# Attention backward on one core: dQ one group later, and other places for the turns of dQ, dK and dV

## The chip, the core and the metric

The kernel runs on one core of one Trainium2 chip, as one launch. The metric is the device time of that launch in microseconds. The core has five engines that run in parallel, each from its own queue of instructions: PE (TensorE, matrix multiplications), ACT (ScalarE, exponentials and copies), DVE (VectorE, elementwise work), POOL (GpSimd) and SP (SyncE, here a queue that issues DMAs). PE writes to PSUM, which the engines read from there; everything else that is computed on lies in SBUF. [...]

## The reference

The reference runs a transformer block with adaptive layer norm forward (S = 2048 tokens, D = 512, H = 32 heads of 16, an MLP with F = 1792) and returns its output and the gradients of nine inputs. What matters here is the gradient of the attention:

```python
scores = jnp.einsum('bhqd,bhkd->bhqk', q, k) * scale
p = _softmax(scores, axis=-1)
o = jnp.einsum('bhqk,bhkd->bhqd', p, v)
...
_out, _vjp = jax.vjp(_f, A_x, A_wqkv, ...)
_grads = _vjp(grad_out)
```

For each head, with P the softmax and dO the gradient of o, the backward pass needs dV = P^T dO, dP = dO V^T, dS = P * (dP - rowsum), dQ = scale * dS K and dK = scale * dS^T Q. The row sums enter through extra columns of dO and V, and the reciprocals of the softmax's sums are folded into dO, so that the kernel uses exp(scores) in place of P.

## The kernel before

The kernel has a forward part, a backward loop over the attention (`attn_bwd`, from about 1166 us to 2390 us of the profiled span) and a last part with the weights' gradients and the gradient of the input. The order in which PE and SP get their instructions is the program's own order, written out by hand; in the backward loop the same holds for POOL.

**Loops.** The backward loop runs over 16 pairs of heads: `g` from 0 to 7 (four heads each) and `jp` 0 or 1. Within a pair, `c` runs over four chunks of 512 keys, `ib0` over four blocks of four query tiles, and `i` over the four tiles of 128 queries in a block. One (`c`, `ib0`) is called a group here, and `m` (0 to 15) is its number within the pair; there are 256 groups in all. One (group, `i`) is a unit.

**A unit.** PE computes the scores of both heads (L1586, into a `st` tile of PSUM, three of them), ACT takes the exponential (L1589, into `pu`, six of them). One unit later, PE computes dP (L1511, into `dp`, three PSUM tiles) and DVE multiplies it by `pu` (L1515) into `ds`, of which there are three, each for one group. In groups with an odd `m` (`off`), one of the eight products is done otherwise: ACT copies dP to SBUF (L1523) and POOL multiplies (L1524). Units then wait in the list `pend`, and some units later `kv` adds their parts of dK and dV on PE into the single PSUM tile `acckv` (L1455). At the end of each chunk `c` ACT evicts `acckv` to `kvT` (L1458).

**dQ.** dQ needs dS transposed. When the last unit of a group is in `ds`, SP issues a DMA that transposes the group into a `dsT` buffer (L1532); in groups with an even `m`, four of its 32 blocks are transposed by PE at `i == 2` of the group itself and copied over by ACT instead (`turn_ds`, L1545 and L1546). There are four `dsT` buffers. The group's eight dQ steps (a step is four matmuls of `dq`, L1478, into the PSUM tile `accq`) go into the list `pendq`, which is served at `i == 0` and `i == 2` of each group:

```python
elif i % 2 == 0 and len(pendq) > 4 * G:
    for _ in range(8 if len(pendq) > 6 * G else 4):
        dq(pendq.pop(0))
```

With G = 4, a group's steps join the list at `i == 0` of the next group, and are worked off at `i == 0` and `i == 2` of the third group after it. After a pair's last step DVE evicts `accq` to `dqT` (L1483); the next pair's first dQ step writes the same PSUM tile.

**Turns.** At the end of a pair dK and dV lie in `kvT`, and dQ in `dqT`, with the head's elements along the partitions. A turn transposes them on PE and copies them to their places on ACT: for dK and dV two turns, each of eight transposes (L1468) and two copies (L1472); for dQ one turn of four transposes (L1491) and one copy (L1492). Turns wait in the list `turnq`; at `i == 3` of any group one of them is taken, if there is one. So a pair's turns are done in the first groups of the next pair.

**Loads.** POOL's queue brings the heads' next K, Q, V and dO in pieces (L1575), about one in each group, after a small copy (`tick`, L1574) that waits for the latest `ds`. In the last two pairs the pieces are weights and the normed input for the part after the loop.

Of the kernel before, what the change touches and what calls it, by code (L numbers as in the profile page):

```python
# [105 lines left out]
class K:  # L106
# [1322 lines left out]
    def attn_bwd(self):  # L1429
# [8 lines left out]
        S, D, H, NQ, ST, SC = self.S, self.D, self.H, self.NQ, self.ST, self.SC  # L1438
        G = 4
# [7 lines left out]
        pend, pendq, turnq = [], [], []  # L1447
# [12 lines left out]
        def turn(g, jp, kvT, s0):  # L1460

            if kvT is None:
                return turn_q(g, jp)
            h0 = 4 * g + 2 * jp
            n = ST // 2
            tp = stp.tile([P, n, P], BF16, name="st")
            for st in range(n):
                nc.tensor.transpose(tp[:, st, :], kvT[:, (s0 + st) * P:(s0 + st + 1) * P], self.ident[:])  # L1468
            v = tp[:].rearrange("p s (t a e) -> p t s a e", t=2, a=2)
            for t, dst in enumerate((self.dk_t, self.dv_t)):  # L1470
                d = dst[:, s0:s0 + n, h0 * DH:(h0 + 2) * DH].rearrange("p s (a d) -> p s a d", a=2)
                nc.scalar.copy(d, v[:, t, :, :, 0:DH])  # L1472

        def dq(u):
            (T, g, jp, c, ib0, a, sub, dsT) = u
            col = 32 * (2 * jp + a) - DH * a
            for i in range(G):
                nc.tensor.matmul(accq[32 * i:32 * i + 32, ib0 // G, :], lhsT=T["K"][:, 4 * c + sub, col:col + 32],  # L1478
                                 rhs=dsT[:, (i * 2 + a) * 4 + sub, :],
                                 start=(c == 0 and ib0 == 0 and a == 0 and sub == 0), stop=False,  # L1480
                                 skip_group_check=True)
            if (c, ib0, a, sub) == (SC - 1, ST - G, 1, 3):
                nc.vector.tensor_scalar(self.dqT[:], accq[:].rearrange("p b q -> p (b q)"), self.scale, None, ALU.mult)  # L1483
                turnq.append((g, jp, None, 0))
# [9 lines left out]
        def kv_two(n=2):  # L1494
            for _ in range(n):
                u = pend.pop(0)
                kv(u)
                (T, g, jp, c, ib, kvT, pu, ds) = u
                if ib < ST - 1:
                    continue  # L1500
                if c % 2 and (g, jp) == (NQ - 1, 1):
                    turnq.append((g, jp, kvT, 4 * (c - 1)))
                elif c == SC - 1:
                    turnq.extend((g, jp, kvT, s0) for s0 in (0, ST // 2))

        def dP(u, a):

            (T, g, jp, c, ib, kvT, pu, dsg, i, grp) = u
            rd = slice(64 - 64 * jp, 128 - 64 * jp)
            dp = dpp.tile([P, 512], F32, name="dp")  # L1510
            nc.tensor.matmul(dp[:], lhsT=T["dOT"][rd, ib * P:(ib + 1) * P],  # L1511
                             rhs=masked["VT"][a][rd, 512 * c:512 * (c + 1)], start=True, stop=True)
            if a == 1 and i == 1 and off(c, ib):
                return dp
            nc.vector.tensor_tensor(dsg[:, i, a], dp[:], pu[:, a, :], ALU.mult)  # L1515

        def off(c, ib):
            return (c * SC + ib // G) % 2 == 1

        def dP_pool(u, dp):  # L1520
            (T, g, jp, c, ib, kvT, pu, dsg, i, grp) = u
            f = (self.junk6, self.csq)[(c * SC + ib // G) // 2 % 2]
            nc.scalar.copy(f[:], dp[:])  # L1523
            nc.gpsimd.tensor_tensor(dsg[:, i, 1], f[:], pu[:, 1, :], ALU.mult)  # L1524

        def dS(u):

            (T, g, jp, c, ib, kvT, pu, dsg, i, grp) = u
            pend.append((T, g, jp, c, ib, kvT, pu, dsg[:, i]))
            if i == G - 1:  # L1530
                dsT, n = grp
                nc.sync.dma_start_transpose(dsT[:, n:, :], dsg[:].rearrange("p i a k -> p (i a k)")[:, n * P:])  # L1532
                for a in range(2):
                    for sub in range(4):
                        pendq.append((T, g, jp, c, ib - G + 1, a, sub, dsT))

        def turn_ds(dsg, grp, skip):

            dsT = dtp.tile([P, 8 * G, P], BF16, name="dsT")
            grp.extend((dsT, 0 if skip else 4))  # L1540
            if skip:
                return
            tp = stp.tile([P, 4, P], BF16, name="st")
            for b in range(4):
                nc.tensor.transpose(tp[:, b, :], dsg[:, 0, 0, b * P:(b + 1) * P], self.ident[:])  # L1545
            nc.scalar.copy(dsT[:, 0:4, :], tp[:])  # L1546
# [4 lines left out]
        for g in range(NQ):  # L1551
            for jp in range(2):
                if jp == 0:
                    if g + 1 < NQ:
                        Tn, later = self.load_group(g + 1)
                    else:
                        Tn, later = None, self.wq_pieces(1) + self.load_wmt()
                    cut = len(later) // 2 if Tn else len(later)
                    pieces = self.pair_pieces(g, 1) + later[:cut]
                    later = later[cut:]  # L1560
                elif g + 1 < NQ:
                    pieces = self.pair_pieces(g + 1, 0) + later
                else:
                    pieces = [(self.xhat1_6[:, st, :], self.xhat1_d.rearrange("(st p) d -> p st d", p=P)[:, st, :])
                              for st in range(ST)]
                kvT = kvp.tile([P, S], BF16, name="kvT")
                total = len(pieces)
                for c in range(SC):
                    c0 = 512 * c
                    for ib0 in range(0, ST, G):  # L1570
                        m = c * (ST // G) + ib0 // G
                        while pieces and (total - len(pieces)) * SC * ST <= m * G * total:
                            if last:
                                nc.gpsimd.tensor_copy(tick[:], last[7][0:1, 0, 0, 0:1])  # L1574
                            nc.gpsimd.dma_start(*pieces.pop(0))  # L1575
                        dsg, grp = self.dsp.tile([P, G, 2, 512], BF16, name="ds"), []
                        for i in range(G):
                            ib = ib0 + i
                            q = slice(ib * P, (ib + 1) * P)
                            if turnq and i == 3:  # L1580
                                turn(*turnq.pop(0))
                            pu = self.pup.tile([P, 2, 512], BF16, name="pu")
                            for a in range(2):
                                stt = stp.tile([P, 512], F32, name="st")
                                rs = slice(64 * jp, 64 * jp + 64)
                                nc.tensor.matmul(stt[:], lhsT=T["QT"][rs, q], rhs=masked["KT"][a][rs, c0:c0 + 512],  # L1586
                                                 start=True, stop=True)
                                held = dP(last, a) if last else None
                                nc.scalar.activation(pu[:, a, :], stt[:], ACT.Exp, scale=self.scale)  # L1589
                                if held is not None:  # L1590
                                    dP_pool(last, held)
                                if a == 0 and i % 2 == 1 and off(c, ib) and len(pend) >= 4:
                                    kv_two(1)
                            if last:
                                dS(last)
                            last = (T, g, jp, c, ib, kvT, pu, dsg, i, grp)
                            if i % 2 == 1 and len(pend) >= 4:
                                kv_two(1 if off(c, ib) else 2)
                            elif i % 2 == 0 and len(pendq) > 4 * G:
                                for _ in range(8 if len(pendq) > 6 * G else 4):  # L1600
                                    dq(pendq.pop(0))
                            if i == 2:
                                turn_ds(dsg, grp, off(c, ib))
            T = Tn
# [341 lines left out]
```

## Time and profile before

| | |
|---|---|
| runs of the kernel before | 2515.72 us median of 3 (2510.71 to 2517.65) |
| the profiled execution's own time | 2515.11 us |
| its span in the trace | 2513.3 us, 76903 instructions |
| granted TensorE clock | 0.998 of full speed |
| PE, ACT, DVE, POOL busy | 97%, 91%, 68%, 28% of the span |
| the backward loop | 1166 to 2390 us, about 76.5 us a pair |

Busy shares are of the whole span, and are no measure of one stage: DVE is at 68% overall, and at 9 tenths or more in every slice of the backward loop. A row of the groups of instructions gives the line, the engine, what is written from what, the count, the busy time and the mean duration, and then the idle time of the engine just before such instructions, with the instruction whose end released it. Durations of instructions in a row on ACT and DVE overlap, so that the distance from start to start is shorter than the duration. A wait row gives the waiting engine and line, what it waited for, the sum, the number of waits and the longest. A DMA's row on SP shows how long its issue took there; the time to landing is shown separately.

### The profile page before, as it was taken

How to read it: one execution, taken by the hardware profiler on the slowest of the kernel's cores; microseconds unless marked ns; L12 is line 12 of the kernel's file. 1: busy time of each engine (PE TensorE's matmuls, PEld its weight loads, DVE VectorE, ACT ScalarE, POOL GpSimd, SP SyncE). 2: the span in 40 equal slices, each digit the busy share in tenths (PEclk: the TensorE clock that was granted, in tenths of full speed). 3: DMA queues.
4: the chain of work that ended last, by engine and by line, in shares of the span. 5: the costliest groups of instructions: out<-in, count | busy, mean ns of one | idle time of the engine just before them, and what ended most of it. 6: DMA issues, size and time to landing. Idle time of an engine off the chain costs nothing.

```text
span 2513.3 us, 76903 instructions
## 1 busy us (share of the span) xinstructions
PE 2437.6 (97%) x30791; PEld 1133.6 (45%) x30791; DVE 1708.5 (68%) x3519; ACT 2297.0 (91%) x3773; POOL 715.9 (28%) x1289
## 2 busy tenths in 40 slices
PE   8999999999999999999999999999999999999998
PEld 4555555555555554673333333333333333333343
DVE  6222323422332333677999999999999999999957
ACT  7999999999999997535999999999999999999935
POOL 2344531321131022255222222222222222222223
PEclk9999999999999999999999999999999999999999
DMA  4589661441343044699999999999999999999997
GB/s 166 135 180 206 173 117 67 112 100 45 102 118 75 24 134 134 133 203 210 233 225 218 219 228 221 228 227 219 221 221 226 227 224 219 227 224 231 237 191 205
DMA packets 1260558, 446.30 MB, mean 178 GB/s; under 512 B 1204052, under 2 KB 1228246, under 8 KB 1260198
## 3 DMA queue, kind: packets, MB, share of 16 engines
q1 hardware_dynamic: 1219654, 336.29, 71.5%
q0 software_dynamic: 38464, 104.04, 13.7%
q8 instruction: 241, 3.95, 0.6%
q10 hardware_dynamic: 2080, 1.05, 0.1%
q14 instruction: 119, 0.97, 0.1%
HBM read 75.83 MB, written 64.49 MB: 56 GB/s over the span
## 4 chain that ended last, share of the span: by engine, by line
PE 55%; ACT 24%; DMA 12%; issue 4%; DVE 3%; POOL 0%; SPq 0%; DVEq 0%; ACTq 0%; POOLq 0%
ACT pu L391 19%; PE st L1586 15%; DMA dsT<-ds 10%; PE st L388 8%; PE acckv L1455 7%; PE accq L1478 5%; ACT pu L1589 4%; PE accbank L322 3%; DVE ds L1515 2%; PE dps L1050 2%; PE pps L1237 2%; PE dp L1511 1%; PE st L1545 1%; PE dps L995 1%; PE pps L631 1%
## 5 line engine op out<-in xcount | busy, mean ns | idle before, releaser
L1515 DVE TENSOR_TENSOR ds<-dp,pu 128x512 bf16<-128x512 f32 x1920 | 1180.5, 684 | 33.2 <-PE dp L1511 26.4
L1589 ACT ACTIVATE pu<-st 128x512 bf16<-128x512 f32 x2048 | 1075.3, 657 | 34.6 <-PE st L1586 21.3
L391 ACT ACTIVATE pu<-st 128x1024 bf16<-128x1024 f32 x992 | 912.1, 1077 | 2.9 <-PE st L388 2.7
L388 PE MATMUL st<-QTm,KTq 128*128 128x512 bf16 x1984 | 587.7, 377 | 19.5 <-ACT pu L391 6.0
L322 PEld LDWEIGHTS <-pu 128*128 128x128 bf16 x8192 | 347.5, 96 | 235.7 <-issue 2.5
L1511 PE MATMUL dp<-kvm,q 64*128 64x512 bf16 x1024 | 363.5, 384 | 1.3 <-DVE g2w L1056 0.7
L1511 PE MATMUL dp<-kvm,dOTg 64*128 64x512 bf16 x1024 | 362.2, 384 | 0.0
L322 PE MATMUL accbank<-Vaug,pu 128*128 128x17 bf16 x8192 | 357.7, 171 | 1.2 <-ACT Vaug L522 0.9
L1586 PE MATMUL st<-kvm,q 64*128 64x512 bf16 x1024 | 349.9, 381 | 4.7 <-ACT pu L1589 0.2
L1586 PE MATMUL st<-kvm,QTg 64*128 64x512 bf16 x1024 | 349.4, 381 | 4.0
L388 PEld LDWEIGHTS <-KTq 128*128 128x128 bf16 x1984 | 188.1, 96 | 176.1 <-issue 124.4
L1524 POOL TENSOR_TENSOR ds<-junk,pu 128x512 bf16<-128x512 f32 x64 | 73.9, 1154 | 370.3 <-ACT junk L1523 284.1
L1455 PE MATMUL acckv<-ds,Qg 128*16 128x512 bf16 x1024 | 176.2, 382 | 0.0
L1455 PE MATMUL acckv<-pu,dOg 128*16 128x512 bf16 x1024 | 175.9, 382 | 0.0
L1455 PE MATMUL acckv<-pu,q 128*16 128x512 bf16 x1024 | 175.8, 382 | 0.0
L1455 PE MATMUL acckv<-ds,q 128*16 128x512 bf16 x1024 | 175.8, 382 | 0.0
L1524 POOL TENSOR_TENSOR ds<-csq,pu 128x512 bf16<-128x512 f32 x64 | 73.8, 1153 | 354.5 <-ACT csq L1523 354.5
L302 POOL DMA_DIRECT2D QTm<-QTq_d x124 | 63.3, 512 | 340.8 <-PE st L388 320.0
L1586 PEld LDWEIGHTS <-q 64*128 64x128 bf16 x1024 | 66.9, 93 | 141.0 <-issue 108.8
L1586 PEld LDWEIGHTS <-QTg 64*128 64x128 bf16 x1024 | 66.6, 93 | 141.0 <-issue 108.0
L329 DVE RECIPROCAL rl<-accbank 128x4 f32<-128x4 f32 x128 | 23.0, 179 | 157.4 <-PE accbank L322 157.2
L1478 PE MATMUL accq<-dsT,Kg 128*32 128x128 bf16 x4096 | 105.5, 221 | 10.5 <-DMA dsT<-ds 10.2
(387 smaller groups left out, 3168.2 us busy)
## 6 DMA issues: line engine op xcount, KB each, us to landing
KTq<-KTq_d POOLq DMA_DIRECT2D x24, 512.0 KB, 3.7
duT_d<-auT POOLq DMA_DIRECT2D x3, 1792.0 KB, 7.7
aT_d<-rT POOLq DMA_DIRECT2D x3, 1792.0 KB, 11.1
KTq_d<-KTq SPq DMA_DIRECT2D x32, 128.0 KB, 2.2
QTq_d<-ev_fm SPq DMA_DIRECT2D x32, 128.0 KB, 4.3
ktm_d<-ev_tm POOLq DMA_DIRECT2D x32, 128.0 KB, 2.6
VTq_d<-vT POOLq DMA_DIRECT2D x4, 1024.0 KB, 6.3
dsT<-ds SPq DMA_TRANSPOSE x256, 6.9
```

Source lines behind the costliest of these rows:

```text
L302: nc.gpsimd.dma_start(QTm[j][32 * j:32 * j + 32, :], self.QTq_d[g, 32 * j:32 * j + 32, 512 * qc:512 * (qc + 1)])
L322: nc.tensor.matmul(acc[:, a, sub, :], lhsT=pu[:, a, sub * P:(sub + 1) * P], rhs=Vaug[:, kb, h, :], start=(kb == 0 and a == 0 and sub == 0) ...
L388: nc.tensor.matmul(stt[:, a, :], lhsT=KT[:, kb * P:(kb + 1) * P], rhs=QTm[2 * jp + a][:], start=True, stop=True)
L391: nc.scalar.activation(pu[:], stt[:], ACT.Exp, scale=self.scale)
L1050: nc.tensor.matmul(pt[:], lhsT=a[st], rhs=g_tm[:, st, :], start=(st == 0), stop=(st == ST - 1))
L1455: nc.tensor.matmul(acckv[r:r + DH, :], lhsT=T[n][:, ib, col:col + DH], rhs=src[:, a, :], start=(ib == 0), stop=(ib == ST - 1))
L1478: nc.tensor.matmul(accq[32 * i:32 * i + 32, ib0 // G, :], lhsT=T["K"][:, 4 * c + sub, col:col + 32], rhs=dsT[:, (i * 2 + a) * 4 + sub, :], ...
L1511: nc.tensor.matmul(dp[:], lhsT=T["dOT"][rd, ib * P:(ib + 1) * P], rhs=masked["VT"][a][rd, 512 * c:512 * (c + 1)], start=True, stop=True)
L1515: nc.vector.tensor_tensor(dsg[:, i, a], dp[:], pu[:, a, :], ALU.mult)
L1524: nc.gpsimd.tensor_tensor(dsg[:, i, 1], f[:], pu[:, 1, :], ALU.mult)
L1586: nc.tensor.matmul(stt[:], lhsT=T["QT"][rs, q], rhs=masked["KT"][a][rs, c0:c0 + 512], start=True, stop=True)
L1589: nc.scalar.activation(pu[:, a, :], stt[:], ACT.Exp, scale=self.scale)
```

## The change

A variable `lag` takes the place of the constant 4 in the rule for `pendq`: it is 6 in all pairs but the last, where it stays 4. With 6, a group's dQ steps are worked off in the fourth group after it instead of the third. The number of `dsT` buffers stays four. In the last pair, the first two groups have steps of eight in place of four until the list is down to its old length.

A turn is taken only from a certain group of the pair on: one of dK and dV from `m` = 2, one of dQ from `m` = 7. Before, the dK and dV turns came at `m` = 1 and 2 (the last `kv` of a pair is done at `i == 3` of the next pair's group 0), and the dQ turn at `m` = 3; now they come at 2, 3 and 7. Since dQ itself ends a group later, the eviction of `accq` moves from `m` = 2 to `m` = 3.

```diff
                 kvT = kvp.tile([P, S], BF16, name="kvT")
+                lag = 4 if (g, jp) == (NQ - 1, 1) else 6
                 total = len(pieces)
...
-                            if turnq and i == 3:
+                            if turnq and i == 3 and m >= (7 if turnq[0][2] is None else 2):
                                 turn(*turnq.pop(0))
...
                             if i % 2 == 1 and len(pend) >= 4:
                                 kv_two(1 if off(c, ib) else 2)
-                            elif i % 2 == 0 and len(pendq) > 4 * G:
-                                for _ in range(8 if len(pendq) > 6 * G else 4):
+                            elif i % 2 == 0 and len(pendq) > lag * G:
+                                for _ in range(8 if len(pendq) > (lag + 2) * G else 4):
                                     dq(pendq.pop(0))
```

## The prediction

> **What bounds the kernel now.** I read the page's busy shares first (PE 97%, ACT 91%, DVE 68%), then its slices: from slice 18 on PE, DVE and ACT all show 9, so the backward loop, about 1166 to 2390 us, is the stretch to look at. Within it a table of windows gives, of 1220 us, PE 1195, ACT 1205 and DVE 1186 busy. Then the groups of instructions:
>
> ```profile
> L1515 DVE TENSOR_TENSOR ds<-dp,pu 128x512 bf16<-128x512 f32 x1920 | 1180.5, 684 | 33.2 <-PE dp L1511 26.4
> L1589 ACT ACTIVATE pu<-st 128x512 bf16<-128x512 f32 x2048 | 1075.3, 657 | 34.6 <-PE st L1586 21.3
> ...
> L1478 PE MATMUL accq<-dsT,Kg 128*32 128x128 bf16 x4096 | 105.5, 221 | 10.5 <-DMA dsT<-ds 10.2
> ```
>
> Columns: busy us and mean ns | idle before, with its releaser. DVE and ACT each have one large group and almost no idle time; the reader should notice that what idles them comes from PE, and that PE itself is idle for a DMA at L1478. The waits of PE, ACT and DVE inside the loop (us, times, longest):
>
> ```profile
> PE accq L1478 <- DMA dsT<-ds: 15.1, 29, 1.3
> ...
> ACT pu L1589 <- PE dp L1511: 8.1, 15, 1.2
> ...
> DVE ds L1515 <- PE dp L1511: 26.3, 56, 1.2
> ```
>
> dQ waiting for its transposed dS is PE's only wait with a named cause. By windows it is 9.9 us up to 2231, 2.7 in the pair from 2231 to 2309 (pair 15) and 2.5 in the last pair. The tile view of dsT:
>
> ```profile
> L1532 SPq DMA_TRANSPOSE dsT<-ds x256: 3433/4162/6181, 1173.0 to 2389.8; - x128
> ...
> DMA to landing us min/median/max: 5.3/6.9/9.7
> ```
>
> From starts in the trace: the first dQ matmul of a group comes 8.1 us (median) after the issue of its transpose. A landing of up to 9.7 us misses that: this is the 1.3 us of lateness.
>
> Next the turns, in ACT's timeline of one pair (start, length, what). L1546 and L1523 are the one copy that each group makes at i = 2, so from one to the next is one group:
>
> ```profile
> 1626.19 0.59 ACT L1546 COPY dsT<-st 128x512 bf16<-128x512 bf16 x1
> ...
> 1631.06 0.70 ACT L1523 COPY junk<-dp 128x512 f32<-128x512 f32 x1
> 1631.53 0.51 ACT L1472 COPY dk_t<-st 128x256 bf16<-128x256 bf16 x1
> ...
> 1636.11 0.62 ACT L1546 COPY dsT<-st 128x512 bf16<-128x512 bf16 x1
> 1636.58 0.43 ACT L1472 COPY dk_t<-st 128x256 bf16<-128x256 bf16 x1
> ...
> 1641.29 0.59 ACT L1523 COPY csq<-dp 128x512 f32<-128x512 f32 x1
> 1641.75 0.62 ACT L1492 COPY dq_t<-st 128x512 bf16<-128x512 bf16 x1
> ...
> 1646.58 0.59 ACT L1546 COPY dsT<-st 128x512 bf16<-128x512 bf16 x1
> ```
>
> and DVE at the same place:
>
> ```profile
> 1631.74 4.97 DVE L1515 TENSOR_TENSOR ds<-dp,pu 128x512 bf16<-128x512 f32 x8 [0.58 <-PE dp L1511]
> 1636.63 0.68 DVE L1483 TENSOR_SCALAR dqT<-accq 128x512 bf16<-128x512 f32 x1
> 1637.23 4.27 DVE L1515 TENSOR_TENSOR ds<-dp,pu 128x512 bf16<-128x512 f32 x7
> 1641.85 2.58 DVE L1515 TENSOR_TENSOR ds<-dp,pu 128x512 bf16<-128x512 f32 x4 [0.36 <-PE dp L1511]
> ```
>
> So today the turns fall in groups 1 and 2 (dK, dV) and 3 (dQ). The three intervals are 5.05, 5.18 and 5.29 us; the same places later in the pair take 4.49, 4.62 and 4.67 (copies at 1651.45, 1655.94, 1660.56, 1665.23). The turns cost 0.56, 0.56 and 0.43 (0.62 less a DMA wait of 0.19), 1.55 us a pair; ACT's share by start-to-start distances is 0.53, 0.53 and 0.48. In group 1 DVE idles 0.58 for the turn. In group 2 it does not, because the eviction of accq (L1483, +0.60 from its start to the next) stands in the same place.
>
> Even groups give DVE 8 multiplications, odd ones 7 (the eighth goes to POOL). At 0.598 us from start to start that is 4.78 and 4.19; ACT has 8 x 0.478 + 0.466 = 4.29 in either. DVE binds even groups, ACT odd ones.
>
> **What the Trainium skill says.** "Perfetto Trace Analysis", Identifying the Most-Contended Engine: matmul busy share is no measure, for Scalar and Vector occupancy is; hence I use ACT and DVE, and the trace bears it out, since PE's 97% still leaves its stalls to reach both. Same page, Optimizing Scalar/DVE Operations: an instruction's profiled time overlaps the next one's by its write acknowledgement; here 684 ns against a distance of 598 (L1515), 657 against 478 at the tightest (L1589), so I count distances. Same page, Summary of the profiler window: of a hardware-queue DMA the window leaves out the data movement; here 4.16 us on SP against 6.9 to landing. "DMA: Bandwidth & Descriptors", Issuing engines are not separate DMA queues: loads from another queue interleave on the same 16 engines. The trace agrees: the last two pairs, with the largest loads, have 5.2 us of waits in 154, against 9.9 in the 1065 before.
>
> **The change part by part.** Nothing is added or removed on any engine. The built instruction order has SP and POOL unchanged, dQ one group later on PE, the turns' copies moved on ACT, the eviction L1483 moved on DVE.
>
> *dQ one group later.* The deadline of a landing goes from 8.1 to 8.1 + 4.6 = 12.7 us; the longest recorded is 9.7. So PE's wait ends in all pairs but the last, where the lag is 4 as today: 15.1 - 2.5 = 12.6 us. How much reaches the end: the 256 groups took 14 us more in sum than if each had taken the median of its place in the pair; 14/15.1 = 0.93, so 11.7. What is late next: the ds ring of three. DVE's first write into a reused ds buffer also waits for that transpose, and comes 1.0 us after dQ did, at 9.1 us. Two of 64 recorded landings are above 9.1, and with the longest wait at 1.3 little is left: I give back 0.9 (none to 3). **-10.8.** The dsT ring: the buffer is freed by dQ at i = 2 and taken by L1546 at the same i = 2; the copy follows transposes that stand behind that dQ on PE, so ACT's exponentials behind it wait for nothing new. POOL's loads of K come in the second pair of a group from its group 4 on, the last dQ of the old K ends in group 3 of the first: no wait. Both at nothing.
>
> *Catching up in the last pair.* Groups 0 and 1 hold 4 more dq steps each, 16 matmuls that take 0.34 us from start to next start. The first pair has one group less of them, where PE is not the limit. Between 0 and 0.7; **+0.3.**
>
> *Turns and eviction.* Group 1 loses its turn: -0.56. The dK/dV turn in group 2 now stands alone, in a DVE-bound group where ACT has 4.62 - 4.29 = 0.33 to spare: between 0.2 and 0.53, I take 0.25. In group 3 the second turn stands beside the eviction, as group 2 has it today: 0.56 (0.15 if the eviction fills DVE's idle time in an odd group and the turn ACT's spare time). The dQ turn in group 7 is as in group 3 now: 0.43 (0.1 to 0.48). New sum 0.25 + 0.52 + 0.43 = 1.2, taking 0.52 for group 3 as the odd group is lighter for DVE; gain 0.35 a pair (0 to 1.1). There are 15 pairs with turns; the last keeps its eviction in group 2, so 14.5: **-5.1** (+1 to -13).
>
> Sum -15.6. Against the profiled execution's own 2515.1 (span 2513.3 and 1.8 around it) that gives 2499.5; the median of the runs is 0.6 higher, so 2500.
>
> **Rivals.** *The turns gain nothing*: each costs its ACT time wherever it stands. For: they cost 0.56 and 0.43 now, near their full 0.53 and 0.48, even where ACT had slack. Against: those places had no DVE backlog. 2515.7 - 10.5 = 2505.
>
> *The wait moves to the ds ring, or the transposes are short of rate and not of time*, so a later deadline only lets them fall further behind. For: DMA slices at 9 throughout. Against: SP itself waits for DVE before 219 of the 256 transposes, which a queue with a backlog would not. Turns and catch-up alone: 2515.7 - 4.8 = 2511.
>
> *Slower*: the eviction in front of the next pair's dQ, now between groups 3 and 4. Today L1483 ends 0.95 us before that dQ starts. With both a turn and the seven multiplications ahead, it decides once DVE falls a further 0.95 us behind PE; then PE waits up to the eviction's 0.68 in each of 15 pairs, and the turn in group 2, with no cover, idles DVE 0.58: 1.26 x 15 = 19, less 10.8: 2524. Against it: the odd group is the one where DVE has most room.
>
> *The change does not do what it says* is excluded by the instruction order.
>
> **Numbers.** Both parts as summed 0.64; turns at nothing 0.20; ds ring or rate 0.12; slower 0.04. A measurement of this kernel tells about 0.3%, 7.5 us, from no change: faster means below 2508.2. That takes 0.62 + 0.19 + 0.03 = 0.84; within 0.3% 0.12; slower 0.04. Range: from DMA at 12.6 and turns at 12 (2491) to the ds-ring case (2510).
>
> **What would show it.** Right: PE's wait at L1478 falls to about 2.5 us, nearly all after 2300; DVE's idle time falls with it; intervals of groups 1, 2, 3 and 7 near 4.5, 4.9, 5.2 and 5.1. Wrong: a wait of DVE at L1515 for a dsT landing (ds ring); a wait of PE at L1478 on L1483 (slower rival); intervals of 2, 3 and 7 longer by the full 0.5 each.

## The result, and the profile after

The changed kernel takes 2526.19 us (median of 18 runs, 2515.53 to 2543.11) against 2516.44 for the kernel before (18 runs, 2510.71 to 2527.45): a ratio of 1.004, 95% interval 1.0023 to 1.0057. It is some 10 us slower, where 16 less were forecast, and its runs scatter more. Its profiled execution took 2524.76 us, with a span of 2522.6.

The two large groups on the page of the changed kernel (busy us, mean ns | idle before, releaser):

```profile
L1515 DVE TENSOR_TENSOR ds<-dp,pu 128x512 bf16<-128x512 f32 x1920 | 1181.2, 682 | 42.3 <-DMA dsT<-ds 16.5
L1590 ACT ACTIVATE pu<-st 128x512 bf16<-128x512 f32 x2048 | 1072.6, 661 | 28.2 <-PE st L1587 22.1
```

The work is what it was. What is new is DVE's releaser: it was PE's dP and is now the landing of a transpose. The waits in the changed kernel's loop up to 2385 us, of PE, then DVE, then ACT (us, times, longest):

```profile
PE dp L1511 <- DVE ds L1515: 14.3, 25, 1.6
...
DVE ds L1515 <- DMA dsT<-ds: 16.5, 24, 2.0
DVE ds L1515 <- PE dp L1511: 12.4, 45, 0.6
...
DVE ds L1515 <- PE acckv L1455: 3.2, 6, 0.6
DVE ds L1515 <- PE st L1587: 2.8, 3, 1.2
...
ACT dsT L1546 <- PE st L1545: 14.1, 22, 2.2
```

PE's wait at L1478, 15.1 us before, is gone from this list. In its place DVE waits 16.5 us for the same transposes, where it wants to write into a ds buffer that one of them still reads. PE then waits for DVE, and ACT waits for PE: L1546, the copy that each even group makes at `i == 2`, needs PE's transposes of the group's first ds slice, which is the very slice that DVE could not write. ACT's only row in the kernel before was 8.1 us; now L1546 alone has 14.1.

The 16.5 us are not all of it. By the trace DVE waits at the first write into a group's ds buffer in nine more places, 5.9 us in sum, which the view puts down to PE (all six at `acckv`, two of the three at L1587) or, once, to ACT. Where the landing of the transpose concerned is recorded, in one of the nine, DVE starts 0.12 us after it, just as it does in the seven recorded waits that the view puts down to the DMA. Taken as landings too, these make 22.4 us in 33 waits.

One such place, in the timeline of DVE and then of ACT:

```profile
2033.90 2.58 DVE L1515 TENSOR_TENSOR ds<-dp,pu 128x512 bf16<-128x512 f32 x4
2038.16 3.68 DVE L1515 TENSOR_TENSOR ds<-dp,pu 128x512 bf16<-128x512 f32 x6 [1.69 <-DMA dsT<-ds]
```

```profile
2034.01 4.28 ACT L1590 ACTIVATE pu<-st 128x512 bf16<-128x512 f32 x8
2039.98 0.58 ACT L1546 COPY dsT<-st 128x512 bf16<-128x512 bf16 x1 [1.70 <-PE st L1545]
2040.47 1.09 ACT L1590 ACTIVATE pu<-st 128x512 bf16<-128x512 f32 x2
```

DVE idles 1.69 us for a landing and ACT 1.70 us behind it: here the wait passes through whole. The exponentials that stand behind L1546 in ACT's program start only after it, at 2040.47. The tile view of dsT in the changed kernel (issue on SP in ns, min/median/max; then landing):

```profile
L1532 SPq DMA_TRANSPOSE dsT<-ds x256: 3482/4368/6627, 1175.7 to 2403.3; - x128
...
DMA to landing us min/median/max: 5.4/7.6/10.2
```

The median issue went from 4162 to 4368 ns and the median landing from 6.9 to 7.6 us. From the trace: the mean issue is 4.26 us before and 4.53 now, and of the 256 transposes 57 before and 154 now were issued over 0.15 us after their last product on DVE was ready, because SP was still at the one before. So the transposes are not only waited for elsewhere: they come later. By the trace the loop, from the first to the last exponential, is 1221.9 us before and 1232.6 now.

The delay of the issue is what the ds ring has no room for. Counted from the issue, two of the 64 recorded landings are above 9.1 us, the same number as before. Counted from the end of the group's last product on DVE, which an issue in time follows by 0.06 us, 15 of the 64 are above 9.15 us, against 3 before. Of the 33 transposes that DVE waited for, 30 were issued late, and the mean delay of all 33 is 1.2 us.

### The profile page after: what moved, and what is told of

Its sections match the earlier page's. It is cut to its first block, busy times and chain, and to the rows that moved or that the text cites. A ratio compares the mean times of both kernels' runs of the same rounds, so it can differ in the third digit from the quotient of the medians.

```text
span 2522.6 us, 76901 instructions
## 1 busy us (share of the span) xinstructions
PE 2449.2 (97%) x30791; PEld 1130.8 (45%) x30791; DVE 1710.2 (68%) x3519; ACT 2298.4 (91%) x3773; POOL 714.0 (28%) x1289
## 4 chain that ended last, share of the span: by engine, by line
PE 54%; ACT 24%; DMA 13%; issue 4%; DVE 3%; POOL 1%; SPq 0%; DVEq 0%; ACTq 0%; POOLq 0%
ACT pu L391 18%; PE st L1587 15%; DMA dsT<-ds 11%; PE st L388 8%; PE acckv L1455 7%; ACT pu L1590 4%; PE accq L1478 4%; PE accbank L322 3%; PE dps L1050 2%; PE dp L1511 2%; PE pps L1237 2%; DVE ds L1515 1%; PE st L1545 1%; PE dp L1640 1%; PE pps L631 1%
## 5 line engine op out<-in xcount | busy, mean ns | idle before, releaser
L1515 DVE TENSOR_TENSOR ds<-dp,pu 128x512 bf16<-128x512 f32 x1920 | 1181.2, 682 | 42.3 <-DMA dsT<-ds 16.5
L1587 PE MATMUL st<-kvm,q 64*128 64x512 bf16 x1024 | 349.7, 381 | 4.6 <-ACT pu L1590 0.2
L1587 PE MATMUL st<-kvm,QTg 64*128 64x512 bf16 x1024 | 350.2, 383 | 3.9
L1587 PEld LDWEIGHTS <-QTg 64*128 64x128 bf16 x1024 | 66.7, 94 | 142.0 <-issue 108.8
L1587 PEld LDWEIGHTS <-q 64*128 64x128 bf16 x1024 | 66.9, 93 | 141.3 <-issue 109.2
L1511 PEld LDWEIGHTS <-q 64*128 64x128 bf16 x1024 | 89.7, 93 | 53.0 <-issue 46.1
```

## The experiments

Each ratio is to the kernel before, run on the same chip in between, with its 95% interval. "Loop" is the stretch from the first to the last exponential in the profiled execution.

### The two parts alone

dQ one group later, with the old rule for turns:

```diff
-if turnq and i == 3 and m >= (7 if turnq[0][2] is None else 2):
+if turnq and i == 3:
```

> dQ one group later, turns where they were (groups 1, 2, 3). Theory R (the transposes are short of rate; the later dQ takes away the wait of PE that kept them apart, they queue up on SP, and the wait comes back on DVE at the ring of three ds buffers): as slow as the changed kernel, 2520 to 2530 us against 2516, with over 10 us of DVE waiting at L1515 for dsT, and a mean issue of a transpose on SP above 4.4 us (4.26 before, 4.53 in the changed kernel). Theory T (the new places of the turns cost the time): faster than before, about 2505, since the waits at L1478 are gone and the turns are the old ones.

Measured: 2527.09 us, ratio 1.0039 (1.0026 to 1.0053). And the new turns with dQ in the third group:

```diff
-lag = 4 if (g, jp) == (NQ - 1, 1) else 6
+lag = 4
```

> Turns in groups 2, 3 and 7, dQ in the third group after its own as before. Theory R: no change, 2516 within 4 us; PE waits about 15 us at L1478 for dsT, DVE does not wait for it, the mean issue on SP stays near 4.26 us. Theory T: slower, 2522 to 2530 us.

Measured: 2517.67 us, ratio 1.000 (0.9988 to 1.0013), with PE's wait for dsT at 11.8 us, none of DVE, and a mean issue of 4.26 us. With dQ where it was, no cost or gain of the new places of the turns is seen within that interval; the time of the first run is as theory R had it.

Its mechanism is not. Without the new places of the turns DVE waits only 2.2 us for dsT, or 4.6 with the four waits at a first write that the view puts down to PE, where theory R had over 10; the mean issue is 4.36 us. PE's waits in the loop of the kernel with the later dQ alone show another cause, and DVE's row for dsT follows them:

```profile
PE st L1491 <- DVE dqT L1483: 15.2, 14, 1.1
PE dp L1511 <- DVE ds L1515: 3.4, 8, 0.8
...
DVE ds L1515 <- DMA dsT<-ds: 2.2, 5, 0.7
```

With dQ a group later, `accq` is evicted in group 3, and its turn follows at `i == 3` of that same group: PE stands before L1491 until DVE gets to L1483, 1.1 us in each of 14 pairs. (Group 3 takes 5.86 us from copy to copy in the median, 4.87 before.) Before, the dQ turn was third in the queue of turns and came a group later. So the rule `m >= 7` belongs to the later dQ: it takes this wait away. The 0.99 us by which group 3 is longer makes about 14 us in 14 pairs. Different causes stood behind the two equal times, and the totals alone would have hidden that.

### A fourth ds buffer

If the ring of three ds buffers is what is short, a fourth should free the loop. It takes 8 KB per partition, which are not free; they were first won by loading WmT after the loop. The control is the kernel before with that load moved, without the last two lines below.

```diff
...
-later = None, self.wq_pieces(1) + self.load_wmt()
+later = None, self.wq_pieces(1)
...
 wk = self.wkp = self.open_pool("p6w", bufs=1, side="right")
+for piece in self.load_wmt():
+    nc.gpsimd.dma_start(*piece)
...
-self.dsp = self.open_pool("p5ds", bufs=3)
+self.dsp = self.open_pool("p5ds", bufs=4)
```

> Control for the next run: the kernel before, but WmT (1.5 MB in 8 pieces) is loaded after the loop instead of in pair 15, into a pool of the last part, which leaves 12 KB per partition free in the loop. Every theory: waits at L1478 in pair 15 fall from 2.7 us towards 1, the last part may lose up to 5 us; 2511 to 2521.

> The changed kernel with WmT loaded after the loop, and four ds buffers instead of three. Theory N (the ring of three ds buffers alone is what is short; the transposes are late now and then but have rate enough): both deadlines are now above 12 us, no wait for dsT in the loop, 2500 to 2505. Theory R: transposes stay queued on SP with a mean issue of 4.5 us or more, DVE or PE still waits for dsT over 8 us in all, and the time is not below 2512.

Measured: the control 2524.1 us, ratio 1.0021 (1.0011 to 1.0032), worse than expected; the changed kernel with four buffers 2515.89, ratio 0.9993 (0.998 to 1.0006). The totals mix two things. The loop of the latter is 1206.3 us, 15.6 less than before, and PE's waits in it are nearly nothing; DVE has none for dsT:

```profile
PE accq L1478 <- DMA dsT<-ds: 1.6, 2, 1.4
PE dp L1511 <- DVE ds L1515: 0.7, 3, 0.3
```

But the part after the loop grew from 125.0 us to 132.9 in the control and 138.9 here, where the late load stands beside other transfers; in the twelve traces with WmT loaded in the loop it takes 120.0 to 128.9 us. So the forecast gain of the loop is there once ds has four buffers, and is given back by WmT. Of theory R one half stays true here: the mean issue is 4.44 us and 170 transposes were issued late. They queue, but with both deadlines above 12 us (dQ 12.0 and the ds ring 13.4 us after the issue, in the median) it no longer matters.

### The same fourth buffer without moving WmT

WmT's tile is empty until pair 15, so up to there every fourth group can use a view of it as its ds buffer. The first call of `load_wmt` makes the tile alone; its pieces are issued in pair 15 as before.

```diff
...
+self.load_wmt()
+ds4 = self.WmT[:].rearrange("p a b c -> p (a b c)")[:, 0:G * 1024].rearrange("p (i a k) -> p i a k", i=G, a=2)
...
-dsg, grp = self.dsp.tile([P, G, 2, 512], BF16, name="ds"), []
+fourth = m % 4 == 3 and g < NQ - 1
+dsg, grp = ds4 if fourth else self.dsp.tile([P, G, 2, 512], BF16, name="ds"), []
```

> The changed kernel with a fourth ds buffer that costs no memory: up to group 7's pairs every fourth group uses a view of WmT's tile, which is loaded in pair 15 as before. Theory N (what holds the changed kernel back is the ring of three ds buffers: the transposes are later than before, but have rate enough): no wait for dsT up to 2230 us, the loop at about 1208 us as with four buffers and WmT loaded late (1206), and the last part as before: 2500 to 2505 us against 2517, at least 18 below the changed kernel. Theory D (the late load of WmT had relieved the loop, not the buffer): 2515 to 2525, with waits of DVE for dsT as in the changed kernel.

> The same fourth ds buffer in the kernel before, dQ in the third group. Theory N: no change, 2517 within 4 us, since dQ's deadline of 8.1 us is met or missed before that of the ds ring (9.1); PE's wait at L1478 stays at 10 to 16 us. If a longer ds ring helps by itself (theory B), PE's wait falls below 8 us and the time below 2510.

Measured: 2532.4 us, ratio 1.0064 (1.004 to 1.0088), in the changed kernel, and 2551.89, ratio 1.0137 (1.0114 to 1.0159), in the kernel before. Neither theory had that. The tile view of dsT in the former, out of the pool's buffers and out of the view:

```profile
L1535 SPq DMA_TRANSPOSE dsT<-ds x200: 3471/4440/6384, 1174.9 to 2409.7; - x100
...
L1535 SPq DMA_TRANSPOSE dsT<-WmT x56: 4882/5432/7137, 1188.9 to 2252.9; - x56
```

The shortest issue out of the view took 4882 ns. Groups with m = 1, 5, 9, 13 move as many blocks and took 4.90 us on average, those of the view 5.39. The built program has the three ds buffers at multiples of 512 bytes, and the view at 188384, which is 32 bytes short of one. The next two runs move its start by 16 elements, in the line that makes `ds4`:

```diff
-[:, 0:G * 1024]
+[:, 16:16 + G * 1024]
```

> As ring4, but the view begins 32 bytes further on, so that it starts at a multiple of 512 bytes like the three ds buffers (in ring4 it did not, and a transpose out of it took 5.2 to 5.5 us on SP against 4.2 to 5.0). Theory N with alignment: the extra length of those transposes goes, no wait for dsT before 2230 us but in the first pair, loop about 1208 us, total 2500 to 2505. Theory A (alignment does not matter, the place in SBUF does, or the fourth buffer itself): 2525 to 2535 as ring4.

> The aligned fourth ds buffer with dQ in the third group and the old turns. Theory N: 2517 within 4 us with PE's wait at L1478 between 10 and 16 us, since dQ's deadline comes before that of the ds ring. Theory B (a longer ring helps by itself): below 2508.

Measured: 2511.02 us, ratio 0.9965 (0.9952 to 0.9978), with the later dQ; 2522.18, ratio 1.0015 (1.0004 to 1.0025), with dQ in the third group. The view's transposes in the former:

```profile
L1535 SPq DMA_TRANSPOSE dsT<-WmT x56: 4084/4990/6566, 1188.2 to 2230.1; - x56
```

The view's transposes are now like the others: up to pair 14 they take 5.00 us on average, and those of m = 1, 5, 9, 13 take 5.05. With dQ in the third group, where fewer stand queued, the view's mean went from 5.19 to 4.38 us, and that of m = 1, 5, 9, 13 from 4.60 to 4.48. So it was the start of the view, and neither its place in SBUF nor the fourth buffer (theory A).

32 bytes of alignment moved the changed kernel from slower than the one before to faster than it: this version beats both. Its loop is 1215.7 us, and most pairs take the 75.3 us that they take with four buffers; the last two, which have three again, take 78.7 and 80.0. There is little rate to spare in it: 231 of the 256 transposes were issued late, by 3.4 us in the median up to pair 14, and between 1325 and 2225 us PE still waits 3.3 us for them, where none was forecast:

```profile
PE accq L1481 <- DMA dsT<-ds: 1.7, 4, 0.9
PE accq L1481 <- DMA dsT<-WmT: 1.6, 3, 0.7
```

The longer ring alone gains nothing: with dQ in the third group PE still waits 18.3 us at L1481 (L1478 of the other kernels). It needs the later dQ as the later dQ needs it. The forecast of 2500 to 2505 for this version was missed by 6 us or more.

### Shorter transposes

The DMA moves 24 blocks in each group, 8 to 31, instead of 28 or 32.

```diff
-dsT[:, n:, :], dsg[:].rearrange("p i a k -> p (i a k)")[:, n * P:]
+dsT[:, 8:, :], dsg[:].rearrange("p i a k -> p (i a k)")[:, 8 * P:]
...
-rhs=dsT[:, (i * 2 + a) * 4 + sub, :],
+rhs=dsT[:, (max(i, 1) * 2 + a) * 4 + sub, :],
```

> The kernel before with shorter transposes: of each group the DMA moves 24 of the 32 blocks (28 before in even groups), and dQ takes the blocks of i = 1 for those of i = 0; all instructions of the engines stay. Issue on SP near 3.2 us, landing near 5.5. Theory N: PE's wait at L1478 falls from 12 to 15 us below 2, loop about 1209 us, total 2501 to 2506. If the waits are not due to the length of the transposes (theory L, loads alone): wait above 6 us.

> The changed kernel with the same shorter transposes. Theory N: no wait for dsT on PE or DVE, equal to the shortened kernel before within 3 us, so that the whole loss of the change hangs on the landing. Theory P (a later dQ costs on PE or DVE in itself, by its other place beside the rest): slower than the shortened kernel before by 6 to 12 us.

Measured: 2498.57 us, ratio 0.993 (0.9912 to 0.9948), and 2496.84, ratio 0.9924 (0.9905 to 0.9944). With landings at 5.4 us in the median neither waits for dsT (0.2 us, the row below, and nothing), and the two are equal; their loops are 1206.3 and 1205.7 us.

```profile
PE accq L1478 <- DMA dsT<-ds: 0.2, 1, 0.2
```

So when the transposes land in time the change takes 0.6 us off the loop of these two traces and costs nothing, and the whole of its loss hangs on when they land. The loops give the whole account. Late landings cost the kernel before 1221.9 - 1206.3 = 15.6 us, and the changed kernel 1232.6 - 1205.7 = 26.9. The difference, less the 0.6, is the 10.7 us by which the changed loop is longer.

### Without POOL's loads

The loads between the first group of heads and the last are taken away, to see whether it is they that make transposes late.

```diff
+if 1 <= g < NQ - 1:
+    pieces = []
 kvT = kvp.tile([P, S], BF16, name="kvT")
```

> The kernel before without POOL's loads (and tick copies) in the pairs of g = 1 to 6, so these pairs compute with the data of the first two groups of heads. Theory C (the loads, on the same 16 DMA engines, are what makes single transposes late): PE's wait for dsT between 1325 and 2230 us falls from about 7 us below 1.5, total 2503 to 2510. Theory S (transposes are late without them too, by each other): that wait stays above 4.

> The changed kernel without the same loads (g = 1 to 6). Theory C: DVE's wait for dsT in those pairs goes, and the time is that of the kernel before without loads within 3 us. Theory S (once transposes stand queued on SP they stay slow): DVE still waits 5 us or more in those pairs and the mean issue on SP stays above 4.4 us there, total 5 us or more above the kernel before without loads.

Measured: 2511.86 us, ratio 0.997 (0.9961 to 0.998), and 2512.86, ratio 0.9975 (0.9966 to 0.9985): equal, and the former a little above the range given. The waits for dsT between 1325 and 2225 us, first PE's in the kernel before:

```profile
PE accq L1478 <- DMA dsT<-ds: 8.1, 19, 1.2
```

In the changed kernel, where they are DVE's:

```profile
DVE ds L1515 <- DMA dsT<-ds: 11.9, 19, 1.7
```

And PE's in the kernel before without loads:

```profile
PE accq L1478 <- DMA dsT<-ds: 0.8, 2, 0.4
```

The changed kernel without loads has none at all there, and the mean issue in those pairs is 4.02 us in both (4.23 and 4.56 with loads). Between 1325 and 2225 us 28 of the 191 transposes are issued late in each of the two, against 43 of 189 before and 122 of 187 in the changed kernel. It takes both, the loads and the later dQ, to make many of them queue. This is theory C. The `tick` copies went with the loads, and the two were not taken apart.

## Why the prediction was wrong, point by point

**PE's wait at L1478 would go.** Right: it is gone from the list up to 2385 us, and what the trace shows after that is 0.6 us in the last pair, where 2.5 were expected to stay. With four ds buffers, or short transposes, the loop has the length that was forecast for it without waits (11.7 us off the 1221.9 would be 1210; it is 1206).

**What is late next: the ds ring, priced at 0.9 us given back.** This is the step that failed. The ring was named. The number of landings beyond it was taken from the old profile (two of 64 above 9.1 us, none to 3 us in all), as if the transposes would stay when what they are waited by moves. They did not: 154 of 256 were issued late. The count from the issue still gives two of 64; the time that a ring leaves runs from when the group's ds is ready, and from there 15 of 64 are too late. The term measured 16.5 us of DVE waiting in place of 0.9, or 22.4 with the waits at the same place that the view puts down to other engines.

Why they moved, as far as the runs show: a group lasts about 4.7 us and an issue takes 4.26, so SP can win back some 0.4 us a group after a delay by a load. Before, a landing later than 8.1 us after its issue held PE, and with it the next groups' products and the next issues. With dQ out of the way nothing holds them up to the ds ring, and the next transpose is ready while SP is still at the last one. That PE's wait had paced the transposes is argued: no run tests it alone. The kernel with the later dQ alone fits it, since there PE is held at L1491 instead, and 100 transposes were issued late. Why the transposes of the changed kernel are also longer stays open. Its late ones were longer than its punctual ones (odd groups: 4.96 us against 4.55), but with four ds buffers both take the same between 1325 and 2225 us (4.74 and 4.72), and without loads too (4.25 and 4.25).

**The price of a wait that moves.** The ds-ring rival gave 2511, reckoning that at worst the old wait came back. It came back larger. More than ACT's row of 8.1 us had reached the end before: PE's 15.1 us had lengthened the loop by 15.6, close to the prediction's 0.93. Now DVE's 22.4 and the 0.6 us of PE in the last pair go with 26.9; the rest was not traced to single waits.

**Against the rate rival I had held** that SP waited for DVE before 219 of the 256 transposes. That was true before and was no safeguard: in the changed kernel it is 171. Of the rivals this one, the ds ring or the rate, names what happened; its size was too small.

**Turns: -5.1.** They are at nothing (turns alone: ratio 1.000), which is the first rival. The copy-to-copy intervals show which term was wrong. Medians over pairs of the two kernels with short transposes, where no landing disturbs: groups 1, 2, 3 and 7 take 5.06, 5.11, 4.87 and 4.44 us with the old places, 4.49, 5.09, 4.94 and 4.87 with the new. So group 1's relief (0.57), group 3 (4.94, forecast 5.19) and group 7's turn (0.43) came out near or below what was said. Group 2's did not: against the 4.61 of an undisturbed even group its turn costs 0.48, not 0.25. ACT's spare time there does not hide it. The bases were read from one pair, too: groups 3 and 7 without a turn take 4.44, not the 4.67 of the pair shown, so the forecast of group 3 was too high by as much. The price of the dQ turn, 0.43, was right by luck: the 5.29 us of group 3 in the pair shown are 0.42 above the median of 4.87, its base of 4.67 is 0.23 above 4.44, and the 0.19 taken off made up the rest. In sum 19.39 against 19.48 us, 0.09 a pair.

**The eviction in front of the next pair's dQ**, the slower rival: no wait of PE at L1478 on L1483 shows. It was slower for another reason. But a wait on L1483 does exist in the later dQ without the new turns, at L1491 and not at L1478.

**The last pair** was given 0.3 us for catching up. In the two kernels with short transposes it takes 76.2 and 76.4 us; those 0.2 us hold the catching up and the moved turns together.

## What to carry to other kernels

When a consumer is moved later to give a transfer time, every buffer that the transfer touches has a deadline of its own, the source's too: lengthen both rings or neither (four ds buffers alone 1.0015, later dQ alone in its rule of turns 1.004, both 0.9965). Count what a deadline leaves from when the source is ready and not from the issue, since a queued transfer is issued late. Landings read from the old profile did not hold here once the wait was gone; ask whether the queue has time to recover. And test each part alone with its profile, since two parts can each be bad for a different reason and have the same time.

## What the hardware showed that was not expected

The length of a DMA transpose's issue depended on where in SBUF its source begins: out of the same tile, with the same 32 blocks, the median issue was 5432 ns from address 188384 and 4990 ns from 32 bytes further on (a multiple of 512), the shortest 4882 against 4084. Which multiple is needed was not tested. Through the queue on SP that was the difference between ratios of 1.0064 and 0.9965. And loads from another queue lengthened the issue of the transposes: 4.02 us mean issue without them, 4.23 with them in the same pairs of the kernel before.
